# Attention values of two units computed together in every second step, with a third buffer for the turned probabilities

## The chip, the cores and the metric

The kernel runs on one core of a Trainium2 chip. The metric is the device time of one launch in microseconds. Times are medians over runs; the profile is of one execution of its own, so sums are made against that execution.

## What is computed

The reference is a chain of three blocks. The change touches the first, an attention over 2 batches, 8 heads, 576 positions and head dimension 64, with a bias that a small network makes from the positions:

```python
scores = q @ k.T / sqrt(D)                      # per batch and head, 576 x 576
bias = relu((log1p|i-j| / log1p(max(i,1))) * w1 + b1) @ w2
attn = softmax(scores + bias)
x = attn @ v                                    # the "values"
x = (silu(rms(x) @ w_gate) * (rms(x) @ w_val)) @ w_out
out = (s * relu(x @ w_in)**2 + b) @ w_out2
```

All inputs are float32 here except the weights of the two feed-forward blocks, which arrive as 64-bit floats and are split on the chip into a high and a low float32r part.

## The kernel before

The 1152 tokens are cut into 9 tiles of 128 rows, and the 8 heads into 4 pairs. One **unit** `u` is one tile and one pair of heads, so there are 36 units (`NU`), four to a tile. The loop `for s in range(-2, NU + 1)` is a software pipeline written out by hand: no scheduler moves anything (`manual_schedule`), and each engine runs its instructions in the order in which the loop emits them. In step `s` the loop emits, in this order:

- `groups(s)`: for s from 0 to 25 the bias of one group of 16 rows, g = s + 10. TensorE multiplies (`bias_mm`, L184) into one `psB` bank (two for g of 32 and more, so for s from 22 on), ScalarE copies it out (`bias_out`, L200, tile `br`), and SyncE writes it to memory (L204, `rows`). The group of the step before is read back, skewed, by `bias_in` (L218, tile `bias`). A chunk of 8 groups must have landed before unit 8, 16, 24 or 32 can use it.
- `finish_b` in steps with s % 4 == 2: VectorE scales a finished tile (L316 to L319, tile `x`), reading a `psB` bank.
- `scores_mm(s + 1)` (L239): the scores of the next unit for the two heads e = 0, 1, into the two `psA` tiles `a`. There are two such tiles in all, so the scores of one unit wait until VectorE has read those of the unit before.
- `soft(s + 1, 0)` and `soft(s + 1, 1)` on VectorE (L252): scores plus bias and the row maximum, tile `sn`; `expo` on ScalarE (L260): the exponential, tile `pr`.
- `turn_mm(s, 0..2)` on TensorE (L269, L271): the probabilities of unit `s` are turned in three groups of transposes, each in a `psB` bank; `turn_out` copies them to SBUF (L277, tiles `pt0`, `pt1`, `pt2`): `pt0` and `pt2` on ScalarE, `pt1` on VectorE, behind both `soft` of that step.
- in steps with s % 4 == 2 the sum of squares (`finish_s`) on VectorE and a power on GpSimd; in steps with s % 4 == 3 `finish_n`.
- `hide`: the hidden layer of a later bias group (L171, tile `hq`), three of its four parts on VectorE and one on GpSimd from g = 11 on.
- `values_mm(s - 1)` on TensorE (L297): ten matmuls, each of two instructions in the trace, with the turned probabilities of the unit before, into the bank `po`. Units 32 to 35 hold both batches and need twice as many of half the width.
- in steps with s % 4 == 1 `finish_t` (L310) turns a finished tile into a `psB` bank that `finish_b` frees one step later; in steps with s % 4 == 0 `finish_c` (L342) turns it again. `finish_a` (L303, ScalarE) has copied `po` out at the start of the step with s % 4 == 1.
- from step 22 on first steps for the weights of the next block (`TAIL`, `BITS`).

Three `psB` banks go round in order of use: bias, the three turns, `finish_t` and `finish_c` each take the next, so each of these groups waits until the bank that was taken three uses before has been copied out. Everything after the loop is the two feed-forward blocks (L540 to L542).

Of the kernel before, what the change touches and what calls it, by code (L numbers as in the profile page):

```python
# [50 lines left out]
def tile_kernel(ctx: ExitStack, tc: tile.TileContext, q, k, v, ltab, lg, cst, cst2, rms_g, wg, wv, wo, win, wo2, s_p, b_p, out):  # L51
# [3 lines left out]
    def pool(stack, name, bufs, side="left", space=None):  # L55
        kw = {"space": space} if space else {}
        return stack.enter_context(tc.tile_pool(name=name, bufs=bufs, side=side, reuse_waits="tile", **kw))
# [10 lines left out]
    def ring(stack, name, bufs, side="left", space=None):  # L68
        return Ring(pool(stack, name, 1, side, space), bufs)
# [9 lines left out]
    att = ExitStack()  # L79
# [5 lines left out]
    bias_p = ring(att, "bias", 2, "right")  # L85
    sn_p = ring(att, "sn", 2, "right")
    pr_p = ring(att, "pr", 2, "right")
    pt_p = ring(att, "pt", 2, "right")
    dram = pool(att, "dram", 1, space=bass.MemoryType.DRAM)
    tab_p = pool(gen, "tab", 1)  # L90
    h_p = ring(gen, "h", 4 * LEAD)
# [27 lines left out]
    def batches(u):  # L119
        tt = TILES[u // 4]  # L120
        return [tt % 2] if tt < 8 else [0, 1]

    def load_q(p):
        if p < NTT:
            qt[p] = q_p.tile([P, NP, P], F32, name="q")
            nc.sync.dma_start(out=qt[p], in_=q[TILES[p]])

    def load_k(n):
        ks[n] = ac.tile([P, S], F32, name=f"ks{n}")
        nc.sync.dma_start(out=ks[n], in_=k[:, n])  # L130

    def load_v(n):
        t = ac.tile([P, 10, D], F32, name=f"vs{n}")
        nc.sync.dma_start(out=t, in_=v[:, n])
        vs[n] = t
# [74 lines left out]
    def bias_in(g):  # L210
        qc, g16 = divmod(g, 8)
        if qc not in bias:
            bias[qc] = bias_p.tile([P, H, S], F32, name="bias")
        r = rows.pop(g)
        src = bass.AP(tensor=r.tensor, offset=r.offset + 15, ap=[[H * RW - 1, 16], [RW, H], [1, S]])
        for dst in ([0] if qc < 4 else [0, 64]):
            to = dst + (P if qc < 4 else D)
            nc.sync.dma_start(out=bias[qc][dst + g16:to:8 if qc < 4 else 4, :, :], in_=src)  # L218
# [11 lines left out]
    def scores_mm(u):  # L230
        hp = u % 4
        ps = [psA.tile([P, 2, 512], F32, name="a") for _ in range(2)]
        bs = batches(u)
        w = P // len(bs)
        for f in range(2):
            for e in range(2):
                for i, b in enumerate(bs):
                    ed, qc = slice(e * D, (e + 1) * D), slice(i * w, (i + 1) * w)
                    nc.tensor.matmul(ps[e][qc, f, :HF], qt[u // 4][ed, hp, qc],  # L239
                                     ks[b * NP + hp][ed, f * HF:(f + 1) * HF],  # L240
                                     start=True, stop=True, tile_position=(e * D, i * w))
        return ps
# [31 lines left out]
    def turn_out(u, e, pT):  # L274
        w = 512 if e < 2 else P
        t = pt_p.tile([P, w], F32, name=f"pt{e}")
        (nc.vector.tensor_copy if e in PT_DVE else nc.scalar.copy)(t, pT[:, :w])  # L277
        pts[u, e] = t

    def values_mm(u):  # L280
        hp = u % 4
        bs = batches(u)
        if hp == 0:
            pos[u // 4] = psO.tile([P, 512], F32, name="po")
        po = pos[u // 4]
        cols = P // len(bs)
        tl = pts.pop((u, 2))
        pm = [pts.pop((u, e)) for e in range(2)]
        for bi, b in enumerate(bs):
            c0 = bi * cols  # L290
            vt = vs[b * NP + hp]
            for c in range(NQC):
                for e in range(2):
                    dst = po[e * D:(e + 1) * D, hp * P + c0:hp * P + c0 + cols]
                    w, a = (vt[:, 4 * e + c, :], pm[e][:, c * P + c0:c * P + c0 + cols]) if c < 4 else \
                        (vt[:, 8 + e, :], tl[:, c0:c0 + cols])
                    nc.tensor.matmul(dst, w, a, start=c == 0, stop=c == NQC - 1, tile_position=(0, e * D))  # L297
# [3 lines left out]
    def finish_a(p):  # L301
        oT = xx_p.tile([P, DM], F32, name="oT")
        nc.scalar.copy(oT, pos.pop(p))  # L303
        fin[p] = oT
# [8 lines left out]
    def finish_b(p):  # L313
        oT, px = fin[p]
        ri = st_p.tile([P, H], F32, name="ri")
        nc.vector.tensor_scalar(ri, sums.pop(p), 1e-9, None, op0=ALU.add)  # L316
        nc.vector.reciprocal(ri, ri)
        x = xx_p.tile([P, DM], F32, name="x")
        nc.vector.tensor_tensor(out=x.rearrange("p (h d) -> p h d", h=H),  # L319
                                in0=px.rearrange("p (h d) -> p h d", h=H),  # L320
                                in1=ri.unsqueeze(2).to_broadcast([P, H, D]), op=ALU.mult)
        fin[p] = oT, x
# [52 lines left out]
    def bits_of(n):  # L375
        raw, a = wst[n]
        w = wst[n] = wpools["ab"].tile([P, 4 * P], I32, name="ww")
        yield nc.vector.tensor_scalar(a, a, 3, 0x3FFFFFF8, op0=ALU.logical_shift_left, op1=ALU.bitwise_and)  # L378
        yield nc.vector.scalar_tensor_tensor(out=w, in0=raw[:, :, 1], scalar=-0x40000000, in1=a,  # L379
                                             op0=ALU.bitwise_and, op1=ALU.bitwise_or)  # L380
        yield nc.vector.scalar_tensor_tensor(out=w, in0=raw[:, :, 0], scalar=29, in1=w,  # L381
                                             op0=ALU.logical_shift_right, op1=ALU.bitwise_or)
# [15 lines left out]
    NU = 4 * NTT  # L398
# [6 lines left out]
    def hide(g):  # L405
        if g < NG:
            hidden(g)
# [8 lines left out]
    def groups(s):  # L416
        for g in plan[s]:
            pb = bias_mm(g)
            if g == 0:
                pcb = psB.tile([P, 512], F32, name="b")  # L420
                nc.tensor.matmul(pcb[:, 0:1], c2_sb[:, :P], c2_sb[:, P:], start=True, stop=True)
                nc.scalar.activation(cb[:, 0:1], pcb[:, 0:1], AF.Copy, scale=SCALE)
                nc.scalar.activation(cb[:, 1:2], pcb[:, 0:1], AF.Copy, scale=m_sb)
            bias_out(g, pb)
            if g in AHEAD:
                AHEAD[g][0](AHEAD[g][1])
            if s == -2:
                hide(g + LEAD)

    for s in range(-2, NU + 1):  # L430
        r = s % 4
        if s >= 5 and r == 1:
            finish_a(s // 4 - 1)
        if s >= 0 and r == 0:
            load_q(s // 4 + 1)
        if -1 <= s < 4:
            load_k(s + 4)
        if 0 <= s < 6:
            load_v(s + 2)
        landed = list(rows)  # L440
        if s != -1:
            groups(s)
        for g in landed:
            bias_in(g)
        if s >= 6 and r == 2:
            finish_b(s // 4 - 1)
        if s in BITS:
            part = bits_of(BITS[s])
        if 0 <= s + 1 < NU:
            ps = scores_mm(s + 1)  # L450
            if s == -1:
                groups(s)
            soft(s + 1, 0, ps[0])
        next(part, None)
        if 0 <= s < NU:
            turn_out(s, 0, turn_mm(s, 0))
        if 0 <= s + 1 < NU:
            expo(s + 1, 0)
            soft(s + 1, 1, ps[1])
        next(part, None)  # L460
        if 0 <= s < NU:
            for e in (1, 2):
                turn_out(s, e, turn_mm(s, e))
        if 0 <= s + 1 < NU:
            expo(s + 1, 1)
        next(part, None)
        if s >= 6 and r == 2:
            finish_s(s // 4 - 1)
        if s >= 7 and r == 3:
            finish_n(s // 4 - 1)  # L470
        if plan[s] and s >= -1:
            hide(plan[s][-1] + 2)
        if s == 4:
            nc.sync.dma_start(out=g_bc, in_=rms_g.partition_broadcast(P))
            nc.sync.dma_start(out=s_sb, in_=s_p)
            nc.sync.dma_start(out=b_sb, in_=b_p)
        if 0 <= s - 1 < NU:
            values_mm(s - 1)
        if s >= 5 and r == 1:
            finish_t(s // 4 - 1)  # L480
        if s == 6:
            xs = [act_p.tile([P, NKC, NT], F32R, name=f"xs{i}", tag=f"x{i}") for i in range(2)]
        if s >= 8 and r == 0:
            finish_c(s // 4 - 2)
        if s == 26:
            gen.close()
            wpools["ab"] = ring(ctx, "wab", 2)
            wpools["sp"] = ring(ctx, "wsp", 4)
        for at, fn, n in TAIL:
            if at == s:  # L490
                fn(n)
        if s == 34:
            sco.close()
            psC = ring(ctx, "psC", 4, space=PSUM)
# [255 lines left out]
```

## Time and profile before

| | us |
|---|---|
| median of 3 runs | 618.53 |
| lowest, highest | 617.51, 619.91 |
| time of the profiled execution | 618.4 |
| its span, from the first to the last instruction | 616.6 |
| loop of the 36 units, about | 30 to 187 |
| feed-forward blocks, about | 187 to 617 |

So 1.8 us of the profiled execution lie outside its span. PE is TensorE, PEld its weight loads, DVE is VectorE, ACT ScalarE, POOL GpSimd and SP SyncE. A row of the timeline gives the start, the length, the engine, the line and operation, the tiles written and read, their shapes and how many instructions are merged in it. Starts are measured; the ends of matmuls are modelled, so a group of matmuls is measured here from its start to the start of what follows it.

### The profile page before, as it was taken

How to read it: one execution, taken by the hardware profiler on the slowest of the kernel's cores; microseconds unless marked ns; L12 is line 12 of the kernel's file. 1: busy time of each engine (PE TensorE's matmuls, PEld its weight loads, DVE VectorE, ACT ScalarE, POOL GpSimd, SP SyncE). 2: the span in 40 equal slices, each digit the busy share in tenths (PEclk: the TensorE clock that was granted, in tenths of full speed). 3: DMA queues.
4: the chain of work that ended last, by engine and by line, in shares of the span. 5: the costliest groups of instructions: out<-in, count | busy, mean ns of one | idle time of the engine just before them, and what ended most of it. 6: DMA issues, size and time to landing. Idle time of an engine off the chain costs nothing.

```text
span 616.6 us, 11246 instructions
## 1 busy us (share of the span) xinstructions
PE 606.9 (98%) x4368; PEld 544.6 (88%) x4368; DVE 405.3 (66%) x751; ACT 309.3 (50%) x644; POOL 192.5 (31%) x177
## 2 busy tenths in 40 slices
PE   8899999999999999999999999999999999999997
PEld 4366666667779999999999999999999999999997
DVE  7677989987787554565455555447778535878841
ACT  7587877777774444434444223236555325555310
POOL 0342145530122233323432333222233423232420
PEclk9799999999999999999999999999999999999999
DMA  6898445558012122212222231222212321211431
GB/s 199 207 303 250 146 135 156 152 170 227 5 67 69 70 102 104 70 68 103 93 78 70 103 102 70 69 69 102 69 69 94 113 103 51 86 69 68 142 99 51
DMA packets 25877, 67.39 MB, mean 109 GB/s; under 512 B 3136, under 2 KB 4704, under 8 KB 25824
## 3 DMA queue, kind: packets, MB, share of 16 engines
q1 hardware_dynamic: 25776, 66.66, 34.0%
q8 instruction: 34, 0.56, 0.4%
q14 instruction: 19, 0.16, 0.1%
q10 hardware_dynamic: 48, 0.02, 0.0%
HBM read 53.47 MB, written 10.83 MB: 104 GB/s over the span
## 4 chain that ended last, share of the span: by engine, by line
PE 77%; DVE 13%; ACT 5%; issue 3%; DMA 1%; POOL 1%; DVEq 0%; ACTq 0%; POOLq 0%
PE c L541 9%; PE c L542 9%; PE c L540 9%; PE b L542 7%; PE po L297 7%; PE b L541 7%; PE b L540 7%; PE a L239 7%; PE b L269 5%; DVE f L609 5%; DVE hv L605 4%; PE b L184 4%; ACT f L608 3%; PE po L542 2%; PE po L540 2%
## 5 line engine op out<-in xcount | busy, mean ns | idle before, releaser
L394 POOL TENSOR_TENSOR wlo<-ww,whi 128x512 fp32r<-128x512 f32 x68 | 96.0, 1412 | 101.5 <-ACT whi L393 101.5
L372 POOL TENSOR_SCALAR wa<-wa 128x512 f32<-128x512 f32 x68 | 43.9, 645 | 182.8 <-ACT wa L371 180.3
L252 DVE CUSTOM_DVE_ANT_0 sn<-a,bias 128x576 f32<-128x576 f32 x72 | 51.7, 753 | 24.5 <-PE a L239 10.7
L378 DVE TENSOR_SCALAR wa<-wa 128x512 int32<-128x512 int32 x68 | 38.6, 567 | 39.7 <-POOL wa L372 39.7
L371 ACT ACTIVATE wa<-wraw 128x512 f32<-128x512 f32 x68 | 45.3, 666 | 27.9 <-DMA wraw<-in_wo 25.1
L260 ACT ACTIVATE pr<-sn,nm 128x576 f32<-128x576 f32 x72 | 56.2, 780 | 3.5 <-DVE nm L252 3.3
L171 POOL TENSOR_SCALAR hq<-tab,c_sb,thr 128x400 f32<-128x400 f32 (+17 forms) x25 | 46.4, 1864 | 33.6 <-PE b L184 33.6
L541 PE MATMUL c<-f,whi 128*128 128x384 f32 (+1 forms) x168 | 55.7, 332 | 0.0
L542 PE MATMUL c<-f,wlo 128*128 128x384 f32 (+1 forms) x168 | 55.7, 332 | 0.0
L540 PE MATMUL c<-f,whi 128*128 128x384 f32 (+1 forms) x168 | 55.7, 332 | 0.0
L379 DVE SCALAR_TENSOR_TENSOR ww<-wraw,wa 128x512 int32<-128x512 int32 x68 | 52.7, 775 | 3.5 <-DVE wa L378 0.4
L609 DVE SCALAR_TENSOR_TENSOR f<-hv,b_sb,f 128x384 fp32r<-128x384 f32 x48 | 39.2, 817 | 21.9 <-ACT f L608 21.9
L381 DVE SCALAR_TENSOR_TENSOR ww<-wraw,ww 128x512 int32<-128x512 int32 x68 | 50.9, 749 | 2.3
L608 ACT ACTIVATE f<-hv,b_sb 128x384 fp32r<-128x384 f32 x48 | 29.7, 618 | 45.1 <-DVE hv L605 45.0
L239 PE MATMUL a<-ks,q 64*128 64x288 f32 (+1 forms) x320 | 47.6, 432 | 2.4 <-ACT br L200 2.4
L541 PE MATMUL c<-xs,whi 128*128 128x384 f32 x144 | 48.2, 335 | 0.0
L540 PE MATMUL c<-xs,whi 128*128 128x384 f32 x144 | 48.2, 335 | 0.0
L542 PE MATMUL c<-xs,wlo 128*128 128x384 f32 x144 | 48.1, 334 | 0.0
L393 ACT CAST whi<-ww 128x512 fp32r<-128x512 f32 x68 | 41.8, 614 | 12.2 <-DVE ww L381 12.2
L297 PE MATMUL po<-pt,vs 128*64 128x128 f32 (+1 forms) x800 | 47.3, 267 | 0.0
L239 PEld LDWEIGHTS a<-ks,q 64*128 64x128 f32 (+1 forms) x320 | 25.4, 177 | 24.1 <-issue 6.2
L542 PE MATMUL b<-f,wlo 128*128 128x384 f32 (+1 forms) x132 | 44.8, 339 | 0.4 <-POOL wlo L394 0.4
(121 smaller groups left out, 1499.6 us busy)
## 6 DMA issues: line engine op xcount, KB each, us to landing
wraw<-in_wo SPq DMA_DIRECT2D x28, 512.0 KB, 3.2
bias<-rows SPq DMA_DIRECT2D x32, 288.0 KB, 4.3
rows<-br SPq DMA_DIRECT2D x28, 295.5 KB, 2.9
wraw<-in_win SPq DMA_DIRECT2D x16, 512.0 KB, 3.2
wraw<-in_wg SPq DMA_DIRECT2D x12, 512.0 KB, 3.2
wraw<-in_wv SPq DMA_DIRECT2D x12, 512.0 KB, 3.2
vs<-in_v SPq DMA_DIRECT2D x8, 320.0 KB, 7.1
ks<-in_k SPq DMA_DIRECT2D x8, 288.0 KB, 5.9
```

Of the source, the lines that this page charges most:

```text
L239: nc.tensor.matmul(ps[e][qc, f, :HF], qt[u // 4][ed, hp, qc], ks[b * NP + hp][ed, f * HF:(f + 1) * HF], start=True, stop=True, tile_positi ...
L252: nc.vector.tensor_tensor_reduce(out=sn, in0=ps[:, :, :HF], in1=bias[chunk(u)][:, h, :].rearrange("p (f c) -> p f c", f=2), scale=-1.0 / S ...
L260: nc.scalar.activation(prs[u][:, e * S:(e + 1) * S], sn.rearrange("p f c -> p (f c)"), AF.Exp, bias=nm, scale=-1.0, accum_out=sums[u // 4] ...
L297: nc.tensor.matmul(dst, w, a, start=c == 0, stop=c == NQC - 1, tile_position=(0, e * D))
L379: yield nc.vector.scalar_tensor_tensor(out=w, in0=raw[:, :, 1], scalar=-0x40000000, in1=a, op0=ALU.bitwise_and, op1=ALU.bitwise_or)
L381: yield nc.vector.scalar_tensor_tensor(out=w, in0=raw[:, :, 0], scalar=29, in1=w, op0=ALU.logical_shift_right, op1=ALU.bitwise_or)
L394: nc.gpsimd.tensor_tensor(out=lo, in0=w.bitcast(F32), in1=hi.bitcast(F32), op=ALU.subtract)
L540: nc.tensor.matmul(ps, hi[:, ws], ah, start=first, stop=False)
L541: nc.tensor.matmul(ps, hi[:, ws], al, start=False, stop=False)
L542: nc.tensor.matmul(ps, lo[:, ws], ah, start=False, stop=last)
L608: nc.scalar.activation(hh[:, cols(j)], g2, AF.Identity, bias=b_sb)
L609: nc.vector.scalar_tensor_tensor(out=hl[:, cols(j)], in0=g2, scalar=b_sb, in1=hh[:, cols(j)].bitcast(F32), op0=ALU.add, op1=ALU.subtract)
```

## The change

```diff
-    pt_p = ring(att, "pt", 2, "right")
+    pt_p = ring(att, "pt", 3, "right")
...
-        if 0 <= s - 1 < NU:
+        if s >= 2 and s % 2 == 0:
+            values_mm(s - 2)
             values_mm(s - 1)
```

The values of units s - 2 and s - 1 are computed one after the other in even steps, and none in odd steps. Each of the three tiles of turned probabilities gets a third buffer, because unit s - 2 is now read one step later. Nothing else moves: the instructions of VectorE, ScalarE, GpSimd and SyncE stand in the same order as before. What a tensor is called in the rows below differs by a running number only.

TensorE, steps 21 and 22, from the scores of step 21 on (L269 and L271 are the turns, L310 is `finish_t`, L184 the bias, L239 the scores). Before:

```order
L239 MATMUL a<-ks_518,q 128x288 x4
L269 MATMUL b<-ident,pr 128x128 x8
L271 MATMUL b<-ident,pr 128x128
L297 MATMUL po<-pt_1787,vs_520 64x128
...
L297 MATMUL po<-pt_1802,vs_520 64x128 x2
L310 MATMUL b<-ident,oT 128x128 x4
L184 MATMUL b<-hq,c_sb 32x512 x4
L184 MATMUL b<-hq,c_sb 32x16 x4
L239 MATMUL a<-ks_584,q 128x288 x4
```

Now:

```order
L239 MATMUL a<-ks_507,q 128x288 x4
L269 MATMUL b<-ident,pr 128x128 x8
L271 MATMUL b<-ident,pr 128x128
L310 MATMUL b<-ident,oT 128x128 x4
L184 MATMUL b<-hq,c_sb 32x512 x4
L184 MATMUL b<-hq,c_sb 32x16 x4
L239 MATMUL a<-ks_584,q 128x288 x4
L269 MATMUL b<-ident,pr 128x128 x8
L271 MATMUL b<-ident,pr 128x128
L297 MATMUL po<-pt_1777,vs_509 64x128
...
L297 MATMUL po<-pt_1873,vs_586 64x128 x2
```

The values have left the place between the turns and `finish_t`; in step 22 the values of both units stand behind the turns.

TensorE, steps 27 and 28, where no bias is left. Before:

```order
L269 MATMUL b<-ident,pr 128x128 x8
L271 MATMUL b<-ident,pr 128x128
...
L297 MATMUL po<-pt_2229,vs_395 64x128 x2
L239 MATMUL a<-ks_451,q 128x288 x4
```

Now:

```order
L239 MATMUL a<-ks_393,q 128x288 x4
L269 MATMUL b<-ident,pr 128x128 x8
L271 MATMUL b<-ident,pr 128x128
L239 MATMUL a<-ks_451,q 128x288 x4
L269 MATMUL b<-ident,pr 128x128 x8
```

The scores of step 28 now follow the turns of step 27 at once, with no other work of TensorE between them.

## Rows read from the trace of the kernel before

**Rows 1.** The page, busy time of each engine, share of the span, instructions.

```profile
PE 606.9 (98%) x4368; PEld 544.6 (88%) x4368; DVE 405.3 (66%) x751; ACT 309.3 (50%) x644; POOL 192.5 (31%) x177
```

**Rows 2.** Windows: busy us (instructions) of PE, PEld, DVE, ACT, POOL; clock, DMA share, GB/s.

```profile
20.00:40.00 20.00, 18.90 (x145) 10.02 (x145) 13.44 (x34) 14.28 (x33) 8.41 (x5) 0.83 0.88 247
...
30.00:187.00 157.00, 156.35 (x1724) 108.48 (x1722) 129.09 (x309) 119.02 (x288) 51.37 (x36) 1.00 0.54 160
```

**Rows 3.** Timeline, step 0 and the start of step 1, where no values stand yet.

```profile
29.47 1.09 PE L269 MATMUL b<-ident,pr 128*128 128x128 f32 x8
...
30.16 0.58 ACT L277 COPY pt<-b 128x512 f32<-128x512 f32 x1
...
30.40 0.27 PE L271 MATMUL b<-ident,pr 128*128 128x128 f32 x1
...
30.80 0.88 PE L184 MATMUL b<-hq,c_sb 128*32 128x400 f32 x8
```

**Rows 4.** Timeline, steps 7 and 8: `soft` of unit 8, the scores of unit 9.

```profile
61.08 0.76 DVE L252 CUSTOM_DVE_ANT_0 sn<-a,bias 128x576 f32<-128x576 f32 x1 [2.43 <-DMA bias<-rows]
...
61.96 1.85 PE L239 MATMUL a<-ks,q 64*128 64x288 f32 x8
...
63.75 0.44 PE L269 MATMUL b<-ident,pr 128*128 128x128 f32 x2
```

**Rows 5.** Timeline, steps 21 and 22, from the turns of step 21 to those of 22.

```profile
125.31 1.09 PE L269 MATMUL b<-ident,pr 128*128 128x128 f32 x8
...
126.06 0.58 ACT L277 COPY pt<-b 128x512 f32<-128x512 f32 x1 [0.67 <-PE b L269]
...
126.44 1.31 PE L297 MATMUL po<-pt,vs 128*64 128x128 f32 x20
...
126.77 0.69 DVE L277 COPY pt<-b 128x512 f32<-128x512 f32 x1
...
127.69 0.66 PE L310 MATMUL b<-ident,oT 128*128 128x128 f32 x4
128.27 1.11 PE L184 MATMUL b<-hq,c_sb 128*32 128x512 f32 x16
...
129.30 0.69 DVE L319 TENSOR_TENSOR x<-b,ri 128x512 f32<-128x512 f32 x1
129.31 1.24 PE L239 MATMUL a<-ks,q 64*128 64x288 f32 x8
...
130.49 0.98 PE L269 MATMUL b<-ident,pr 128*128 128x128 f32 x7
```

**Rows 6.** Timeline, step 27: its turns, and `soft` of the second head.

```profile
152.64 1.09 PE L269 MATMUL b<-ident,pr 128*128 128x128 f32 x8
...
153.53 0.75 DVE L252 CUSTOM_DVE_ANT_0 sn<-a,bias 128x576 f32<-128x576 f32 x1
```

**Rows 7.** Timeline, steps 33 and 34: turns, values of unit 32, VectorE's queue.

```profile
175.55 1.09 PE L269 MATMUL b<-ident,pr 128*128 128x128 f32 x8
...
176.68 1.39 PE L297 MATMUL po<-pt,vs 128*64 128x64 f32 x40
176.76 0.75 DVE L252 CUSTOM_DVE_ANT_0 sn<-a,bias 128x576 f32<-128x576 f32 x1
...
178.00 0.66 PE L310 MATMUL b<-ident,oT 128*128 128x128 f32 x4
178.04 0.68 DVE L277 COPY pt<-b 128x512 f32<-128x512 f32 x1
...
179.75 0.69 DVE L319 TENSOR_TENSOR x<-b,ri 128x512 f32<-128x512 f32 x1
```

**Rows 8.** Timeline of TensorE, steps 35 and 36: turns of unit 35, values of units 34 and 35.

```profile
182.16 0.66 PE L269 MATMUL b<-ident,pr 128*128 128x128 f32 x4
...
183.69 2.55 PE L297 MATMUL po<-pt,vs 128*64 128x64 f32 x80
186.17 0.33 PE L342 MATMUL b<-ident,x 128*128 128x128 f32 x1
```

## The prediction

> **What bounds the kernel now.** I read the busy shares first, then the windows, then the timeline of the loop step by step. The shares put TensorE at 98% of the span [rows 1], and in the loop it is busy 156.35 of 157 us at full clock [rows 2]. Ends of matmuls are modelled, so I checked starts: from step 1 to step 34 each group of matmuls starts where the one before it is through, and TensorE waits once, in step 8, for a transfer [rows 4]. The reader is to see in rows 5 that the turns, the values, `finish_t`, the bias, the scores and the next turns follow each other without a gap, while the copies of VectorE and ScalarE lie beside them. So TensorE sets the end of the loop, nothing of its work is hidden, and a wait that the change puts on it counts in full. The feed-forward blocks behind the loop are the same kind of stretch, with TensorE as bound; they only start earlier or later.
>
> **The gain: fewer changes between groups.** Two units of values in one run save one change between kinds of matmul. Before, the last two units already stand so: 80 instructions take 186.17 - 183.69 = 2.48 us [rows 8], where one unit of that shape takes 178.00 - 176.68 = 1.32 [rows 7]. So a pair saves 2 x 1.32 - 2.48 = 0.16 us. Of 18 pairs 17 are new: 17 x 0.16 = 2.7 us. For the wider units no pair is in the trace; the bounds are zero and 0.20, the time from the last turn to the next group (the turns, 1.13 us in rows 5, less the 30.40 - 29.47 = 0.93 to the last of them in rows 3). I take 0.16, the pair that was measured. One wait goes as well: the turns of unit 35 to the values take 183.69 - 182.16 = 1.53 us [rows 8] instead of 1.13, because they follow the short step 34 and find the exponential late. Now two more values (1.2 us) stand ahead of them: 0.4 saved. The third buffer costs nothing: the copies into it have less to wait for.
>
> **The cost: what the values hid.** In odd steps the 1.25 us of values (127.69 - 126.44, rows 5) no longer stand between the turns and what comes next. Three banks go round, so the next group needs the bank of the first turn, copied out on ScalarE, the one after it that of the second, copied out on VectorE behind both `soft`, and so on. I put each release as a distance from the start T of the turns of the odd step.
>
> (a) *First bank.* T = 125.31: the copy ends at 126.06 + 0.58 = T + 1.33, the turns are through at T + 1.13 [rows 5]. A wait of 0.20. Step 0 of the kernel before has no values either and shows just this: turns at 29.47, copy to 30.74, bias at 30.80, so T + 1.33 again [rows 3]. This hits `finish_t` (s % 4 == 1) or the bias (s % 4 == 3).
>
> (b) *Second bank*, in odd steps with `finish_t` and a bias after it. `finish_t` takes 128.27 - 127.69 = 0.58, so from T + 1.33 it is through at T + 1.91; the copy on VectorE ends at 126.77 + 0.69 = T + 2.15 [rows 5], and with 0.06 from a copy's end to TensorE's start (30.80 - 30.74, rows 3) the bias starts at T + 2.21. A wait of 0.30.
>
> (c) *Bank of `finish_t`*, freed by `finish_b` at 129.30 + 0.69 = T + 4.68. In step 22 the bias has two banks, so the first turn comes round to it: from T + 2.21, 1.04 of bias (129.31 - 128.27) and 1.18 of scores (130.49 - 129.31) give T + 4.43 [rows 5]. A wait of 0.3. With a one-bank bias it is the second turn, half a microsecond later, which no longer waits.
>
> (d) *Scores without a bias between*, steps 27 and 31. `soft` of the second head ends at 153.53 + 0.75 = T + 1.64 with T = 152.64 [rows 6]; the scores want its tile at T + 1.13. 0.51, with the 0.06 of a handover 0.57: together 1.1 us.
>
> (e) *Steps 33 and 34*, where VectorE also does weight work. T = 175.55: 0.20 at `finish_t`; the scores reach T + 1.91 and wait for 176.76 + 0.75 + 0.06 = T + 2.02; (the second `soft`); with the 1.18 of scores from (c) they end at T + 3.20, where the first turn waits for the copy on VectorE, 178.04 + 0.68 + 0.06 = T + 3.23; the last turn, 0.93 on, is at T + 4.16 and needs the bank of `finish_t`, free at 179.75 + 0.69 + 0.06 = T + 4.95 [rows 7]. Together 0.20 + 0.11 + 0.03 + 0.79 = 1.1 us.
>
> (f) *Up to step 8.* Here the waits don't add. Unit 8 needs a transfer that lands at 61.08 on VectorE, whatever TensorE does, and the scores of unit 9 take 63.75 - 61.96 = 1.79 instead of 1.18 for it [rows 4]. TensorE arrives early and waits longer, and leaves with the values of unit 6 still owed: 1.25 less 0.16. To that comes what delays the transfer itself, whose group is computed in step 5: two waits of (a) less two pairs, 0.1. So 1.2 us after step 8.
>
> **The sum.** 1.2 for (f). Behind step 8, (a) falls on 10 odd steps (9 to 25, and 29; 27, 31 and 33 are counted apart): 2.0. (b) falls on 9, 13, 17 and 21: 1.2. (c) 0.3, (d) 1.1, (e) 1.1. That is 6.9. Against it 13 pairs behind step 8, 2.1, and the 0.4 of unit 35. Net 4.4 us: 618.4 + 4.4 = 622.8 for the profiled execution, which stands 0.1 below the median of the runs, so I use it for both.
>
> **Bounds.** Low: the savings at 0.20 a pair (2.6), (b) at half, (c) and 0.6 of (e) hidden because VectorE comes earlier after the longer even steps: 1.2 + 2.0 + 0.6 + 1.1 + 0.5 - 2.6 - 0.4 = +2.4, 620.8. High: a pair saves only 0.10 (1.3), and ScalarE, which in odd steps with s % 4 == 1 also copies `po` (0.59 us) and the bias out, is 0.1 later in each of the 10 steps: 6.9 + 1.0 - 1.3 - 0.4 = +6.2, 624.6.
>
> **Rivals.** *No wait appears, faster.* The bank of the first turn is what decides: were it free at T + 1.13 instead of T + 1.33 the odd steps would lose nothing there, and with the others covered only the saving stays: -2.7 - 0.4, 615.3. Rows 3 speak against it, since the kernel before shows the wait where no values stand. 0.04.
>
> *The waits are there, but VectorE is ahead.* After an even step of two values VectorE has had 1 us more to clear its queue. If `soft` and the copy come 0.3 earlier in odd steps, (b), (c) and much of (d) and (e) go: 1.2 + 2.0 + 0.5 + 0.6 - 2.5 = +1.8, 620.2, within what counts as the same. Against it: in rows 5 the copy starts at 126.77, T + 1.46, which two `soft` of 0.75 each [rows 6], a little overlapped, fill from T on, and they cannot begin before the scores are through at T. 0.13.
>
> *TensorE is not the limit at all.* Weight loads fill 108.48 of the loop's 157 us [rows 2], so TensorE might have a third of its time to spare, and then neither saving nor waits would move the end: 618.4. The Trainium skill, page Perfetto Trace Analysis, section Identifying the Most-Contended Engine, says that matmul busy time is a poor measure of headroom and weight-load busy share a better one; by that rule this rival would be likely. The starts in rows 5 speak against it: no group has room before it. 0.06.
>
> *VectorE becomes the bound.* It is busy 129.09 of 157 us [rows 2]. In short odd steps it may not keep up, so its copy and `soft` come some 0.3 later in nine steps: +2.7 on the forecast, 625.5. 0.10.
>
> *The clock falls.* In the window from 20 to 40 us the granted clock is 0.83 [rows 2]: (1 - 0.83) x 20 / 0.5 = 6.8 us at the lower level, 1.2 GHz, after TensorE had waited there. If the new waits do that once in the loop, half the work of 6.8 us is lost: 622.8 + 3.4 = 626.2. But the new waits are under 0.8 us each, and the one of 0.6 in rows 4 left the clock at 1.00. 0.05.
>
> **Numbers.** Forecast 622.8 with 0.62. About 0.5% (3.1 us, from 615.4 to 621.6 around the runs) is what a measurement of this kernel can tell from no change. Faster by more: 0.04, the first rival. Same: 0.13 + 0.06 and 0.06 from the lower end of the forecast, 0.25. Slower: 0.71. The range that should hold 8 in 10 leaves out the first and the third rival and parts of the second and of the last: 620.0 to 626.2.
>
> **What would show it.** In the profile after: groups of 40 values in even steps that take 2.34 us to the next start; in odd steps the bias or `finish_t` 1.33 us after the start of the turns, and the bias after `finish_t` at 2.2; scores in steps 28 and 32 about 1.6 to 1.7 after the turns of the step before; the last turn of step 34 late by 0.8; the scores of unit 9 begun at the same 62 us as before with one unit less of values done; the feed-forward blocks unchanged in length. It is wrong if the turns in odd steps are followed at 1.13 us, or if waits appear in even steps.

## The result and the profile after

The changed kernel takes 623.12 us (median of 6 runs, 621.68 to 624.50) beside 618.55 for the kernel before (6 runs, 617.51 to 619.91). The ratio is 1.007, with a 95% interval of 1.0045 to 1.0095: slower by 0.7%. The profiled execution took 623.88 us with a span of 622.1, which is 5.5 us above the span of before. All of it lies ahead of the feed-forward blocks: from their first matmul to the end of the span it is 430.0 us in both (622.1 - 192.08 and 616.6 - 186.58).

The page of the changed kernel, busy time of each engine, against [rows 1]:

```profile
PE 606.9 (98%) x4368; PEld 548.1 (88%) x4368; DVE 405.0 (65%) x751; ACT 309.4 (50%) x644; POOL 193.3 (31%) x177
```

TensorE's busy time is the same, and only the span has grown. The windows (columns as in [rows 2]) say where TensorE now stands idle:

```profile
20.00:40.00 20.00, 16.49 (x117) 9.59 (x119) 12.72 (x33) 12.77 (x31) 8.25 (x5) 0.83 0.94 268
30.00:187.00 157.00, 152.39 (x1599) 105.05 (x1599) 126.01 (x303) 116.76 (x282) 50.26 (x33) 0.99 0.53 155
```

4.6 of 157 us are now without a matmul, where it was 0.65 [rows 2]. The timeline shows the places. First steps 21 and 22, against [rows 5]:

```profile
128.00 1.09 PE L269 MATMUL b<-ident,pr 128*128 128x128 f32 x8
...
128.69 0.58 ACT L277 COPY pt<-b 128x512 f32<-128x512 f32 x1 [0.62 <-PE b L269]
...
129.33 0.66 PE L310 MATMUL b<-ident,oT 128*128 128x128 f32 x4
...
129.46 0.69 DVE L277 COPY pt<-b 128x512 f32<-128x512 f32 x1
...
130.20 1.11 PE L184 MATMUL b<-hq,c_sb 128*32 128x512 f32 x16 [0.22 <-DVE pt L277]
...
131.24 1.24 PE L239 MATMUL a<-ks,q 64*128 64x288 f32 x8
...
131.99 0.69 DVE L319 TENSOR_TENSOR x<-b,ri 128x512 f32<-128x512 f32 x1
...
132.73 1.09 PE L269 MATMUL b<-ident,pr 128*128 128x128 f32 x8 [0.25 <-DVE x L319]
```

With T = 128.00: `finish_t` starts at T + 1.33, 0.06 after ScalarE's copy ends (128.69 + 0.58 = 129.27). The bias starts at T + 2.20, right behind VectorE's copy (130.15), and the turns of step 22 at T + 4.73, right behind `x` (132.68). The row names the releaser in brackets. Three banks are wanted one after the other, and each is given back a little too late.

Steps 27 and 28, where the scores follow the turns, against [rows 6]:

```profile
156.17 1.09 PE L269 MATMUL b<-ident,pr 128*128 128x128 f32 x8
...
157.06 0.75 DVE L252 CUSTOM_DVE_ANT_0 sn<-a,bias 128x576 f32<-128x576 f32 x1
...
157.30 1.81 PE L239 MATMUL a<-ks,q 64*128 64x288 f32 x8
...
159.04 1.09 PE L269 MATMUL b<-ident,pr 128*128 128x128 f32 x8
```

The scores begin on time, T + 1.13, with the first head, and stand in their middle until the second `soft` ends at 157.81: 1.74 us from their start to the next turns, where 1.17 is the usual length. Step 31 shows the same (1.69 instead of 1.13).

Steps 33 to 36, against [rows 7, 8]:

```profile
179.96 1.09 PE L269 MATMUL b<-ident,pr 128*128 128x128 f32 x8
...
181.29 0.66 PE L310 MATMUL b<-ident,oT 128*128 128x128 f32 x4
...
181.88 1.29 PE L239 MATMUL a<-ks,q 64*64 64x288 f32 x16
...
183.28 1.06 PE L269 MATMUL b<-ident,pr 128*128 128x128 f32 x8
...
183.57 0.64 POOL L372 TENSOR_SCALAR wa<-wa 128x512 f32<-128x512 f32 x1 [6.76 <-ACT wa L371]
183.65 0.58 DVE L316 TENSOR_SCALAR ri<-rs 128x8 f32<-128x8 f32 x1
...
184.57 0.69 DVE L319 TENSOR_TENSOR x<-b,ri 128x512 f32<-128x512 f32 x1
...
185.32 0.33 PE L271 MATMUL b<-ident,pr 128*128 128x128 f32 x1 [0.97 <-DVE x L319]
185.57 2.55 PE L297 MATMUL po<-pt,vs 128*64 128x64 f32 x80
188.06 1.09 PE L269 MATMUL b<-ident,pr 128*128 128x128 f32 x8
...
189.19 2.55 PE L297 MATMUL po<-pt,vs 128*64 128x64 f32 x80
```

The last turn of step 34 waits for `x`. The turns of unit 35 reach their values after 189.19 - 188.06 = 1.13 us, without the wait of [rows 8].

Step 7, against [rows 4]:

```profile
61.20 1.09 PE L269 MATMUL b<-ident,pr 128*128 128x128 f32 x8
61.40 0.76 DVE L252 CUSTOM_DVE_ANT_0 sn<-a,bias 128x576 f32<-128x576 f32 x1 [1.57 <-PE a L239]
...
64.35 1.09 PE L269 MATMUL b<-ident,pr 128*128 128x128 f32 x8
```

`soft` of unit 8 is released here by the scores, no longer by the transfer. TensorE came to this place later than before (turns of step 7 at 61.20 instead of 58.94), and the last read of the chunk came a little earlier: issued at 56.44, landed at 60.1, where before it was 57.33 and 60.8. So the transfer was in time.

It came later because of the stretch ahead of the loop. The window from 27 to 34 us, first of before, then of after:

```profile
27.00:34.00 7.00, 6.87 (x52) 3.84 (x46) 7.00 (x18) 6.93 (x18) 5.05 (x3) 0.97 0.90 299
```

```profile
27.00:34.00 7.00, 7.00 (x31) 4.19 (x33) 4.88 (x13) 5.09 (x13) 0.54 (x2) 0.54 0.80 231
```

The granted clock is 0.54 in this window after the change and 0.97 before; in the window from 20 to 27 us it is the reverse (0.97 after, 0.55 before). Up to here TensorE runs the same instructions in both kernels but for the values of unit 0. The lower level (1.2 GHz) came some 6 us later in this execution and fell on denser work (TensorE busy 7.00 of 7 us, where it had been 6.03), and the scores of unit 2 start at 33.25 instead of 31.61. It isn't the change: two kernels below without the pairs have the late form as well (n1 with 33.13 and e7 with 32.90), and one with all the pairs has the early one (n3, 31.85). So the kernels below are compared also by their **loop**: from the start of the scores of unit 2 to the start of the first feed-forward matmul (from there to the end it is 429.9 to 430.1 us in all of them). It takes 154.97 us before and 158.83 after, +3.86; the remaining 1.64 of the 5.5 are the start.

### The profile page after: what moved, and what is told of

Same layout as the page of the kernel before. It is cut to its first block, busy times and chain, and to the rows that moved or that the text cites. A ratio compares the mean times of both kernels' runs of the same rounds, so it can differ in the third digit from the quotient of the medians.

```text
span 622.1 us, 11211 instructions
## 1 busy us (share of the span) xinstructions
PE 606.9 (98%) x4368; PEld 548.1 (88%) x4368; DVE 405.0 (65%) x751; ACT 309.4 (50%) x644; POOL 193.3 (31%) x177
## 4 chain that ended last, share of the span: by engine, by line
PE 74%; DVE 14%; ACT 5%; issue 4%; DMA 1%; POOL 1%; DVEq 0%; ACTq 0%; POOLq 0%
PE c L543 9%; PE c L542 9%; PE c L541 9%; PE po L297 7%; PE b L543 7%; PE b L541 6%; PE b L542 6%; PE a L239 6%; DVE f L610 4%; PE b L269 4%; DVE hv L606 4%; PE b L184 3%; ACT f L609 3%; PE po L543 2%; PE po L541 2%
## 5 line engine op out<-in xcount | busy, mean ns | idle before, releaser
L372 POOL TENSOR_SCALAR wa<-wa 128x512 f32<-128x512 f32 x68 | 43.9, 646 | 185.5 <-ACT wa L371 181.9
L239 PE MATMUL a<-ks,q 64*128 64x288 f32 (+1 forms) x320 | 48.3, 435 | 4.8 <-DVE nm L252 3.4
L239 PEld LDWEIGHTS a<-ks,q 64*128 64x128 f32 (+1 forms) x320 | 26.3, 179 | 26.3 <-DVE nm L252 8.3
L269 PEld LDWEIGHTS b<-ident,pr 128*128 128x128 f32 x288 | 31.5, 143 | 14.9 <-issue 9.3
```

The lines of the kernel that those rows point to most:

```text
L269: nc.tensor.transpose(pT[:, c * P:(c + 1) * P], pr[:, o:o + P], ident)
```

## The experiments

The theory: TensorE is the limit, the values stood where they covered the release of a bank or of a scores tile, and without them TensorE waits by the amounts of (a) to (e). The rivals: the third buffer costs the time; the transfers of the bias, pushed together by uneven steps, cost it; VectorE does. The table gives the ratio to runs of before beside each kernel, and the loop of the profiled execution, in which a step can be followed.

| kernel | median us | ratio [95%] | loop us |
|---|---|---|---|
| before | 618.55 | | 154.97 |
| after | 623.12 | 1.007 [1.0045, 1.0095] | 158.83 |
| e1_buffer | 619.47 | 1.0015 [0.9999, 1.003] | 156.88 |
| e2_pair_r3 | 623.16 | 1.008 [1.0057, 1.0103] | 158.93 |
| e3_pair_r1 | 621.85 | 1.006 [1.0043, 1.0077] | 157.54 |
| e4_twice | 637.07 | 1.0302 [1.028, 1.0323] | 172.44 |
| e5_tail_first | 620.69 | 1.0038 [1.0025, 1.0051] | 155.84 |
| e6_r3_read_first | 627.20 | 1.0143 [1.0098, 1.0187] | 158.69 |
| e7_read_first | 623.34 | 1.0074 [1.0046, 1.0102] | 156.36 |
| e8_all | 623.03 | 1.0088 [1.0058, 1.0117] | 158.01 |
| n1_before | 618.79 | 0.9994 [0.9983, 1.0005] | 153.86 |
| n2_r3 | 621.86 | 1.0042 [1.0029, 1.0056] | 157.05 |
| n3_after | 621.85 | 1.0048 [1.0032, 1.0063] | 158.44 |
| e9_short_first | 616.40 | 0.9961 [0.9949, 0.9974] | 151.63 |

**The buffer alone.** Before, with the ring changed and the values in every step:

```diff
-    pt_p = ring(att, "pt", 2, "right")
+    pt_p = ring(att, "pt", 3, "right")
```

> The third buffer alone, values still in every step. Theory (the loss comes from the waits that TensorE has in odd steps without values): the buffer takes waits away only, so the time is that of before, 618.5 within 0.3%, and the loop reaches the turns of step 1 at a time that scatters as before. Rival (the 1.7 us by which the loop starts later in the profile after belong to the change, by what the larger buffers move in memory): 620.2, with the turns of step 1 at about 34.5 us.

619.47 beside 618.84, and the interval takes in 1. The steps have the lengths of before but for waits in steps 7 (1.6 us, for the chunk of unit 8, as in [rows 4] but longer), 16 (0.6), 23 (0.3) and 34 (0.3). The first two are the transfers': n3 below, with the buffer and without transfers, has neither. The one in step 34, with 0.1 more in step 35, comes with the buffer: 0.4 us, taken up again under (e). As the cause of the 4.6 us the buffer falls.

**Pairs only where the empty step has the bias next.** After, with

```diff
-        if s >= 2 and s % 2 == 0:
-            values_mm(s - 2)
-            values_mm(s - 1)
+        for u in ([s - 2, s - 1] if r == 0 else [] if r == 3 else [s - 1]):
+            if 0 <= u < NU:
+                values_mm(u)
```

(`r` is s % 4), and the same with pairs only behind steps with `finish_t`, that is `[s - 2, s - 1] if r == 2 else [] if r == 1 else [s - 1]`:

> Pairs only in steps with s % 4 == 0, so that only odd steps with s % 4 == 3 are empty; there no finish_t follows the turns. Theory: eight new pairs save 0.15 each (1.2 us); empty steps 3 to 23 wait 0.20 for the first bank (1.2 us), 27 and 31 wait 0.56 for the scores' tile (1.1), step 24 0.1; nothing waits for the second bank behind finish_t, nor for the bank of finish_t. Net +1.2 us, 619.8, between 619.2 and 620.8 by the transfer for unit 8. Rival (every empty step costs the same, 4.6 us / 17 each): 8 of 17, +2.2 us, 620.7. Rival (the waits are hidden by VectorE and ScalarE being ahead): -1.2 us, 617.3.

> Pairs only in steps with s % 4 == 2, so that only odd steps with s % 4 == 1 are empty; there finish_t follows the turns. Theory: nine new pairs save 0.15 each (1.35 us) and unit 35 0.4; the nine empty steps wait 0.20 each for the first bank (1.8), steps 5 to 21 0.29 more for the second (1.45), steps 10 and 22 0.3 for the bank of finish_t (0.65), steps 33 and 34 1.4 more. Net +3.5 us, 622.0. Rival (every empty step costs the same): 9 of 17 of 4.6, +2.4 us, 620.9.

e3 came as expected: the loop is 2.57 us longer than before, and step by step it is the waits of after in its own empty steps (0.20 at the turns of nine, 0.39 and four times 0.29 at `finish_t`, 0.32 in step 22, 0.35 in step 10, 0.27 and 1.17 in 33 and 34: 5.4), less nine pairs (1.4) and the waits of before at steps 7, 8 and 35 (1.5). e2, the half that should have been cheap, missed: its loop is as long as that of after. Four of its eight empty steps (7, 15, 23 and 31) are those just ahead of a chunk's first unit. The timeline of e2 in steps 14 and 15:

```profile
93.28 0.54 SPq L218 DMA_DIRECT2D bias<-rows  x1
...
97.18 1.09 PE L269 MATMUL b<-ident,pr 128*128 128x128 f32 x8
...
98.39 0.76 DVE L252 CUSTOM_DVE_ANT_0 sn<-a,bias 128x576 f32<-128x576 f32 x1 [1.49 <-PE b L271]
```

`soft` of unit 16 starts 1.21 us after the turns instead of 0.2, though the scores it reads were through when the turns began. The last read of its chunk, issued at 93.28, took 4.8 us to land, at 98.0, right ahead of `soft`; the turn named in brackets writes nothing that `soft` reads. The next five kernels take that apart.

**Reading back first.** If SyncE issued the read of the group before ahead of this step's write, the chunk might land earlier. In e2 (as e6) and in the kernel before (as e7):

```diff
-        landed = list(rows)
+        for g in list(rows):
+            bias_in(g)
         if s != -1:
             groups(s)
-        for g in landed:
-            bias_in(g)
```

> Pairs in steps with s % 4 == 0 only, as in e2, but SyncE issues the reading back of the bias group of the step before ahead of the writing of this step's group, not behind it. Theory (what e2 lost over the forecast are the transfers for units 8, 16, 24 and 32, which an empty step with s % 4 == 3 lets TensorE reach 1.1 us earlier): they land sooner by up to 2 us, the extra 3 us go, and what stays is the forecast of e2: 619.8 to 620.4. Rival (the extra loss of e2 is something else in the empty steps): 623.

> The kernel before, but SyncE issues the reading back of the bias group of the step before ahead of the writing of this step's group. Theory: the waits that the kernel before has behind unit 8 (0.6 in step 8 in its profile, 1.6 in that of e1, and 0.6 and 0.3 in steps 17 and 24 there) go: 1 to 2 us less, 617.5. If the transfers were not what holds these steps: 618.6, as before.

Both missed. The kernel before got slower by 0.7%; e6 is 4.0 us above e2 in the median, though its profiled loop is 0.2 shorter. What SyncE's queue waits for between 20 and 190 us (us in total, times, the longest), first before, then e7:

```profile
SPq L218 <- DMA rows<-br: 10.9, 7, 3.0
```

```profile
SPq L218 <- DMA rows<-br: 87.0, 27, 4.5
```

The read needs the write of its group to have landed. Issued early, it stands at the head of the queue until then, and holds up all that follows it there. In the profiled loop of e7 this costs 1.4 us, all of it at unit 16 (steps 15 and 16). The medians differ by 4.8, and that is not this wait alone: three of e7's six runs had a granted clock of 0.994 and took 621.0 to 621.7 us, three had 0.988 or 0.989 and took 625.0 to 625.2. e6 and e8, which also read first, have such runs too, and no other kernel here has a run under 0.991. What lowers the clock in them no trace shows. The place of the read was no slack.

**No reading back at all.** In before (n1), e2 (n2) and after (n3); every unit takes the bias of the first chunk:

```diff
-                                       in1=bias[chunk(u)][:, h, :].rearrange("p (f c) -> p f c", f=2),
+                                       in1=bias[0][:, h, :].rearrange("p (f c) -> p f c", f=2),
...
-        for g in landed:
-            bias_in(g)
```

> The kernel before without the reading back of the bias groups from memory: all units take the bias of the first chunk, so the output is not the reference's. Theory: only the waits behind unit 8 and the later chunks go, 1 to 2 us: 617 to 618. It is the base for n2 and n3.

> Pairs in steps with s % 4 == 0 only, as in e2, without the reading back of the bias (all units take the first chunk's bias). Theory (the loss of e2 over its forecast is the transfers, which an empty step with s % 4 == 3 uncovers): against n1 +1.2 us, the forecast of e2. Rival (the empty steps cost it by themselves): +4 us against n1.

> The changed kernel without the reading back of the bias (all units take the first chunk's bias). Theory: no transfer hides or adds anything, so the whole sum stands against n1: 15 x 0.2 + 5 x 0.3 + 0.65 + 1.1 + 1.5 of waits, 7.8 us, less 17 x 0.15 + 0.4 = 2.95: +4.9 us. Rival (part of the loss in the changed kernel is the transfers): +3 us or less.

n1 is within 0.1% of before: there the transfers cost nothing that the run medians show (1.1 us in the loop, the waits of steps 7 and 8). n3 has nearly the loop of after (158.44 and 158.83), and stands 4.58 over n1: what the change costs in its loop is not the transfers. That rival falls for after. In run medians n3 and n1 differ by 3.1 us; the starts scatter by more than the rest of that gap, but no run settles it. The loop of n2 is 1.9 shorter than that of e2: that much of e2's excess was the transfers. It is still 3.2 over n1, where 1.2 was expected. Of these 2.0 us 0.4 stand in steps 34 and 35, as in e1; the rest is VectorE, in steps 11, 15, 19, 23 (1.0 together) and 31 (0.6). Step 31 of n2:

```profile
170.04 1.09 PE L269 MATMUL b<-ident,pr 128*128 128x128 f32 x8
170.25 0.68 DVE L327 CUSTOM_DVE_ANT_0 oT<-x 128x512 f32<-128x512 f32 x1
...
170.86 0.75 DVE L252 CUSTOM_DVE_ANT_0 sn<-a,bias 128x576 f32<-128x576 f32 x1
...
171.68 1.86 PE L239 MATMUL a<-ks,q 64*64 64x288 f32 x16 [0.43 <-DVE nm L252]
```

An empty step with s % 4 == 3 follows one in which VectorE does `finish_b` and `finish_s` and TensorE has only one unit of values. The sum of squares (L327) still runs when the scores are through, and `soft` comes 0.8 after the turns' start instead of 0.2. After a pair VectorE has the time to clear its queue, so after's own empty steps hardly show this (0.1 in step 23). The forecast's cost for a step with the bias next holds behind a long step, and in n2 only in steps 3 and 7.

**Twice the values.** After, with the values of one unit computed in odd steps too, a second time (the line that lets `values_mm` read the turned probabilities twice is not shown):

```diff
-        if s >= 2 and s % 2 == 0:
-            values_mm(s - 2)
-            values_mm(s - 1)
+        if s >= 1 and (s % 2 == 0 or s < NU - 1):
+            for u in ([s - 2, s - 1] if s % 2 == 0 else [s - 1]):
+                values_mm(u)
```

> Values of one unit in every odd step up to 33 as before, and of two units in every even step, so that the 17 even-numbered units up to 32 are computed twice; the second time writes the same again. Theory: every odd step has its cover again, so the waits are gone, and each extra unit costs a unit in a pair, 1.09 us (1.17 for unit 32): 18.6 us, less the 0.4 of unit 35 and up to 1.0 of waits that before has in step 8: 635.7 to 636.7. If a pair saves nothing, 17 x 1.24 = 21.1 us: 638.2 or more. Rival (TensorE is not the limit in the loop): under 630.

The loop is 17.47 longer than before, for 17 units more. TensorE's timeline of e4, steps 15 and 16:

```profile
103.98 1.31 PE L297 MATMUL po<-pt,vs 128*64 128x128 f32 x20
105.22 0.93 PE L184 MATMUL b<-hq,c_sb 128*32 128x432 f32 x8
...
108.39 2.40 PE L297 MATMUL po<-pt,vs 128*64 128x128 f32 x40
110.72 0.66 PE L342 MATMUL b<-ident,x 128*128 128x128 f32 x4
```

One unit takes 1.24 us, two take 2.33: the third unit of two steps costs 1.09, and next to nothing waits any more (17 x 1.09 less the 1.1 that before waits in steps 7 and 8 is 17.4). So TensorE is the limit in this loop, and anything that gives the banks their time covers the waits. The Trainium skill, page Perfetto Trace Analysis, section Identifying the Most-Contended Engine, would have TensorE's headroom judged by its share of the peak rate and by the busy share of its weight loads. The second is 105.05 of 157 us in the loop after and 108.48 before [rows 2], which by that rule leaves a third to spare. The measurement decides against it here: the added work is paid in full.

**Giving the short bank back first.** If late banks are the cause, the bank with the short copy (the third group of turns, a single transpose) should come round first, and `finish_t` stand ahead of the rest. After, with

```diff
-            turn_out(s, 0, turn_mm(s, 0))
+            for e in (2, 0):
+                turn_out(s, e, turn_mm(s, e))
...
+        if s >= 5 and r == 1:
+            finish_t(s // 4 - 1)
+            finish_b(s // 4 - 1)
         if plan[s] and s >= -1:
```

(the old places of `finish_t`, `finish_b` and group 2 left out):

> The changed kernel, but in each step the short turn (one transpose, whose copy takes 0.25 us) comes first, and finish_t and finish_b are issued ahead of the hidden layer. So behind the turns of an odd step the bank that comes round first is that of the short turn, the second that of the first long turn, and the bank of finish_t is free a microsecond sooner. Theory: the waits for the first bank (15 x 0.2), for the second (5 x 0.3) and for the bank of finish_t (0.66) go, 5.2 us of 6.7; those for the scores' tile in steps 28 and 32 and those of step 34 stay. 617.9, up to 619 where the transfer for unit 8 holds the scores of unit 9. Rival (the loss is not these bank waits): 623.

About half of it came: the loop is 3.0 shorter than that of after. The waits (a), (b) and (c) are gone from nearly all odd steps. But group 2 holds rows of both heads, so it needs the second exponential, and in even steps that comes late: turns to values take 1.25 to 1.56 us there in seven steps (1.13 in after).

**Everything together.** Order 2, 0, 1, early finish, read back first, and pairs only up to step 26:

```diff
+        for u in ([] if s < 1 or s < 26 and s % 2 else [s - 2, s - 1] if s <= 26 else [s - 1]):
+            values_mm(u)
```

> Pairs in even steps up to 26 and single units after that, the short turn first, finish_t and finish_b ahead of the hidden layer, and the reading back of the bias issued first. Theory: 13 pairs save 0.15 each (2.0 us), no bank wait and no transfer wait is left (1 to 2 us less, as in e7), and steps 27 to 34 are as before: 615.0 to 616.0, under both kernels. Rival (the waits of odd steps come back elsewhere, at the scores' tile or at the exponential): 618 or more.

A miss: it carries the cost of reading first (TensorE waits 2.6 us in step 7 and 1.2 in step 15) and of the late exponential in even steps.

**Each where it pays.** The pairs of e8, the early finish, reading back in its old place, and the short group first only where it is wanted:

```diff
+        short = [2] if r == 1 or r == 3 and s < 26 else []
         if 0 <= s < NU:
-            turn_out(s, 0, turn_mm(s, 0))
+            for e in short + [0]:
+                turn_out(s, e, turn_mm(s, e))
```

> Pairs in even steps up to 26, single units after that; the short turn first only in odd steps that no values follow or that finish_t follows, the old order in all others; finish_t and finish_b ahead of the hidden layer. The reading back of the bias stays behind the writing. Theory: e5 gave the waits for the banks back at the turns of even steps, which then needed the second exponential early; here they need it late again. 13 pairs save 2.0 us and no bank wait is left: 615 to 617, under the kernel before. Rival (the transfer for unit 8 or the scores' tile takes it back): 618 or more.

616.40 beside 618.98: 0.4% faster than the kernel before, where after is 0.7% slower. Steps 21 and 22 of e9 on TensorE:

```profile
123.51 0.33 PE L271 MATMUL b<-ident,pr 128*128 128x128 f32 x1
...
123.67 1.04 PE L269 MATMUL b<-ident,pr 128*128 128x128 f32 x8
...
124.55 0.60 PE L310 MATMUL b<-ident,oT 128*128 128x128 f32 x4
...
125.08 1.11 PE L184 MATMUL b<-hq,c_sb 128*32 128x512 f32 x16
...
126.12 1.24 PE L239 MATMUL a<-ks,q 64*128 64x288 f32 x8
...
127.29 1.09 PE L269 MATMUL b<-ident,pr 128*128 128x128 f32 x8
```

The same groups as in the rows of after, from turns to turns: 3.78 us instead of 4.73, with no wait left. In the eight steps with `finish_t` the turns and `finish_t` together even take 1.57 instead of the 1.13 + 0.58 of before. So the loop, 3.34 shorter, is 13 pairs of 0.15 (2.0), 8 times 0.14 (1.1) and the waits of before around steps 7 and 8 (1.1), less 0.9 that still waits, most of it in steps 34 and 35. Why the turns are shorter in that order was not isolated; the four transposes of `finish_t` now follow the eight of group 0 directly.

## Why the prediction was right, and where it wasn't

The forecast of slower was right: 622.8 for 623.12, in the range, for the reason given. The sum held partly by luck. It was 1.15 too high in (f) and did not count 0.50 of a wait of before that goes; against that it was 1.0 too low in (c), (e) and step 23. In the loop 4.4 was forecast and 3.86 came, and the 1.64 at the start isn't the change. Term by term, in the profiled execution (start to start; 5.5 us in all):

| step of the prediction | forecast | measured |
|---|---|---|
| start, up to the scores of unit 2 | 0 | +1.64 |
| (f) from there to the turns of step 8 | +1.2 | +0.05 |
| (a) first bank, 10 steps | +2.0 | +2.0 |
| (b) second bank, 4 steps | +1.2 | +1.14 |
| (c) bank of `finish_t` | +0.3 | +0.32 (step 22), +0.35 (step 10) |
| (d) scores in steps 28 and 32 | +1.1 | +0.57, +0.56 |
| (e) steps 33 and 34 | +1.1 | 0.20 + 0.27 + 1.17 = +1.64 |
| bias to scores in step 23 | none | +0.11 |
| 13 pairs | -2.1 | -1.96 |
| unit 35 | -0.4 | -0.39 |
| wait of before in step 8 | none | -0.50 |

**The wait of before in step 8.** The text took that wait to be over with the scores of unit 9. The row of before shows a second part, which the changed kernel doesn't have:

```profile
67.20 0.74 PE L184 MATMUL b<-hq,c_sb 128*32 128x320 f32 x8 [0.35 <-DVE pt L277]
```

`finish_c` ahead of it takes 1.00 us (66.20 to 67.20) instead of 0.59, and the turns of step 8 1.21 instead of 1.13.

**Pairs, (a), (b), (d) and unit 35** came within a tenth or two of a microsecond. Each had been read as a distance from the turns' start to a copy's or a `soft`'s end, and those distances didn't move when the values left.

**(c) was too small.** The text let only step 22 wait and held that with a one-bank bias the second turn, half a microsecond later, finds the bank free. In step 10 of after it doesn't:

```profile
73.63 0.20 DVE L317 RECIPROCAL ri<-ri 128x8 f32<-128x8 f32 x1
74.31 0.69 DVE L319 TENSOR_TENSOR x<-b,ri 128x512 f32<-128x512 f32 x1 [0.47 <-DVE ri L317]
74.33 0.66 PE L269 MATMUL b<-ident,pr 128*128 128x128 f32 x4
...
75.14 0.63 PE L269 MATMUL b<-ident,pr 128*128 128x128 f32 x4 [0.16 <-DVE x L319]
```

VectorE stands 0.47 us between `ri` and `x`. The trace of before has the same gap at the same place (`x` starts at 73.10 there, T + 4.05, where in [rows 5] it is T + 3.99, although the bias of step 9 is a third shorter). I had read one step of four and taken it for all. n3 shows no such gap (0.10 there), and step 10 loses nothing, so the gap is the cause of this term. It stands in all eight kernels that read the bias back and have `finish_b` in its old place, and in none of the other six. What VectorE waits for in it stays open; the releasers that the profile names (`ri` in after, a bias matmul in before) were through.

**(e) was under-sized by 0.5.** The step that failed is the one that took `x` from [rows 7]: T + 4.89 for its end. It came at T + 5.30, because `ri` (L316) took 0.58 instead of 0.16. That is 0.4 of the 0.5; the rest is small (the scores take 1.13 in this shape and not the 1.18 of (c), the last turn 0.25 and not 0.20). The rows of after show why: GpSimd's instruction of L372 started 0.08 ahead of it and ends 0.02 before it does (184.21 and 184.23). In the kernel before the two start together:

```profile
179.23 0.65 POOL L372 TENSOR_SCALAR wa<-wa 128x512 f32<-128x512 f32 x1 [6.00 <-ACT wa L371]
179.24 0.16 DVE L316 TENSOR_SCALAR ri<-rs 128x8 f32<-128x8 f32 x1
```

The pattern holds in all 14 traces. In the eleven kernels with the third buffer GpSimd leads by 0.07 to 0.12 us, and `ri` takes 0.58 and ends 0.02 to 0.03 behind it; in the three with two buffers (before, e7, n1) it leads by at most 0.013, and `ri` takes 0.16. e1 differs from before by the buffer alone:

```profile
179.81 0.63 POOL L372 TENSOR_SCALAR wa<-wa 128x512 f32<-128x512 f32 x1 [5.94 <-ACT wa L371]
179.89 0.58 DVE L316 TENSOR_SCALAR ri<-rs 128x8 f32<-128x8 f32 x1
```

So the sentence that the third buffer costs nothing failed too: by these traces this is its 0.4 us, and without it (e) would have come to some 1.2. Why the buffer lets GpSimd start earlier stays open. The Trainium skill, page SBUF — State Buffer, section SBUF: two separate sides, says that the two engines share a pair of ports, which VectorE takes in two-port modes or with two inputs in SBUF, and which whoever starts first holds until its instruction ends. The traces agree where GpSimd leads by 0.07 us or more, with 0.42 us as the price here; whether L316 is such an instruction no run shows, and no run was made with the one moved.

**(f) was not put to the test.** It took the landing of unit 8's transfer, 61.08, as fixed, and expected TensorE to wait for it with one unit of values still owed. In the profiled execution the start was 1.64 late, TensorE reached `soft` of unit 8 at 61.40, and no transfer was waited for. The landing was not fixed either: it came at 60.1. In place of +1.2 the stretch shows +0.05, since the new waits there (1.2) just met the pairs and the wait of before. At the absolute time of step 8 the two mistakes partly cancel: 64.35 - 63.75 = 0.60, and 1.09 of values owed, makes +1.7 where +1.2 was forecast. Whether an execution with an early start waits as (f) says, no trace of after shows; e2, which owes the values of unit 6 at the same place, does wait so: its transfer landed at 60.6, and its turns of step 8 start at 63.50, where it is 63.75 before.

**The rivals.** TensorE not being the limit falls by e4, no wait by all rows above. VectorE ahead, or VectorE as the bound, are half a truth each: after a pair it has the time, after a single unit (n2) it hasn't. The clock did move the time, but at the start and in kernels of either kind, not in the loop, where it is 1.00 from 34 to 187 us.

## To carry to other kernels

Before work is taken from a place on the engine that sets the end, list for that place what the next group needs (a bank, a tile, a transfer) and when it comes free; here moving the work saved 0.15 us per pair and uncovered waits of 0.2 to 1.2. Work that needs no free buffer is the cover, so keep it where buffers turn over, and where it must go let the buffer with the shortest copy come round first: that, with `finish_t` and `finish_b` earlier and no pairs in the last steps, turned +0.7% into -0.4%. Read such distances in every step of the pattern, not in one, and see what the step ahead leaves in the queues.

## What the runs showed of the hardware that I had not expected

- TensorE's lower clock level (1.2 instead of 2.4 GHz) comes between 20 and 34 us, for the same instructions at different times: the window from 20 to 27 us has a granted clock of 0.55 in before and 0.97 in after, the next 7 us 0.97 and 0.54, and in e9 both have 0.76. The loop starts between 30.8 and 33.3 us. An effect of 2 us can't be read from one span.
- A VectorE instruction of 0.16 us took 0.58 when an instruction of GpSimd had begun 0.07 to 0.12 us before it (eleven traces), and 0.16 when it had begun at most 0.013 before it (three).
- A read from memory that is issued ahead of the write that it waits behind costs the whole queue: 87.0 us of waiting in 27 pieces in place of 10.9 in 7. It cost 0.7% of the kernel's time in the median, in part by runs with a granted clock of 0.988 or 0.989.
